# A pre-LN block in fp32 on one core: the last token block adds x in two one-pass parts, with its sums, pieces, filler and down weights on other queues and engines

## The chip, the cores and the metric

The kernel runs on one core of one Trainium2 chip. The metric is the time of one execution in device microseconds; a kernel's time is the median of its runs. The core has a matrix engine (PE), a vector engine (DVE), a scalar engine (ACT), GpSimd (POOL) and a sync engine (SP) that here only issues DMAs. Each engine works through its own list of instructions in order and waits on semaphores; ACT and POOL issue DMAs from the same lists. In the rows of the profile "PE" is a matmul, "PEld" its weight load, and "SPq", "ACTq", "POOLq" a DMA being issued.

## The reference

A pre-LN transformer block: attention with 32 query heads and one shared key and value head, then a gated feed-forward part. Sequence 2048, width D = 512, 32 heads of 16, feed-forward width F = 1792, all in fp32.

```python
def _A_ref(x, wq, wk, wv, wo):
    q = (x @ wq).reshape(B, S, H, Dh).transpose(...)
    k = x @ wk
    v = x @ wv
    p = softmax(einsum("bhqd,bkd->bhqk", q, k) * Dh ** -0.5)
    o = einsum("bhqk,bkd->bhqd", p, v)
    return o.transpose(...).reshape(B, S, H * Dh) @ wo

def _B_ref(x, w_gate, w_up, w_down):
    return (gelu(x @ w_gate) * (x @ w_up)) @ w_down

h = x + _A_ref(layernorm(x), wq, wk, wv, wo)
h2 = h + _B_ref(layernorm(h), w_gate, w_up, w_down)
```

## The kernel before

**Tiling.** The 2048 tokens are worked in NB = 4 blocks of T = 512, each of TB = 4 parts of P = 128. A block's attention runs over NG = 8 groups of four heads and KC = 16 key chunks: scores (`s`, L352), exponentials on ACT (`p`, L356) and weighing (`acc`, L360). An `acc` holds, for each of four heads, 16 rows of weighed values and 16 rows that repeat the sum of the exponentials, the divisor.

**Precision.** Matmuls take fp32r operands in one pass; full precision comes from splitting an operand into a high part, the value rounded to fp32r, and a low part, the remainder (`split`, L121: the high part by one engine, the subtraction by the same or another). A product is then hi*hi + hi*lo + lo*hi. Where an operand stays plain fp32, the trace shows two records for one matmul (eight for the four additions of x, L848). The identity `ident` (L102) is fp32; it serves the transposes and, in `add_x` (L847), puts x into the bank of the projection by a matmul of x against the identity.

**What sets the order.** Blocks 0 to 2 are pipelined: while ACT makes the exponentials of block b, a planner (`CYCLES`, L1090 to L1114) weaves in the projection, norm and feed-forward products of block b - 1. A `step` issues the next planned matmul, `available` tells how many can be issued, `catch_up` issues those that are left before a point, `before` and `finish` issue the weighing and the side work due. When fewer products are available than a cycle wants, the cycle is "idle": all available products are issued first. The lists of SP and DVE in this stretch are in program order, not rearranged by the scheduler; those of PE, POOL and ACT are in program order throughout.

**The tail.** The last block has no attention beside it. `rest` (L807) holds back 36 down matmuls of block 2 (token parts 2 and 3, 18 each) as filler for PE. `last_dense` (L818) is a generator that stops at `HOLD`; the driver at L1122 to L1132 runs 18 filler matmuls, goes on to the next HOLD, runs 9, goes on, and then issues the 9 that remain. In `last_dense`:

- L840: x of the last block is loaded into `xp`, four DMAs of 256 KB on SP; then `load_w2` (L515) for the first two pairs of down weights, `w2_3_0` and `w2_3_1`, 1 MB each on SP, into buffers of the same tag `p`.
- The projection `pp` of the first three chunks of 128 channels: 36 matmuls, 9 for each token part.
- Four pieces, one for each token part of the last chunk: `piece(t)` (L409) inverts the divisors, multiplies and splits into `o_hi`, `o_lo`, all on DVE; `add_x(t)`; three matmuls of the last chunk. After piece 2 stands the norm of part 0 (L860), after piece 3 the others. A norm is two statistics instructions on DVE (L132, L133), three small ones on POOL (`rstd`, `shift`, L135 to L143) and one on ACT (`xnp`).
- Transposes (`pxt`, L828), ACT's high part (`x2h`) and DVE's low part (`x2l`), parts 0 and 1 ahead of parts 2 and 3, which use the same two banks.
- Then the feed-forward part: per f of 14 a gate group (`pg`) and an up group (`pu`) of 12 matmuls each, with w1 weights in three buffers: the load issued when a group ends serves the group three further on. `load_w2` at L950 asks for the remaining pairs `w2_3_2` to `w2_3_6`, on SP.

**The last sums.** `evacuate` (L370) copies the last `acc` to `oT` (L373, DVE), and `move_out` (L379) brings its rows to the partitions where the pieces need them: eight DMAs of 32 KB, the divisors' half first, alternating between SP and ACT. The stores of block 2's parts 0 and 1, `out_dram<-h` (L704), are issued by SP after DVE's last h additions (L702).

Of the kernel before, what the change touches and what calls it, by code (L numbers as in the profile page):

```python
# [9 lines left out]
F32 = mybir.dt.float32  # L10
F32R = mybir.dt.float32r
# [8 lines left out]
P = 128  # L20
# [6 lines left out]
PB = 5  # L27
# [30 lines left out]
def kernel(  # L58
# [12 lines left out]
    nc = tc.nc  # L71
# [29 lines left out]

    ident = const.tile([P, P], F32, name="ident")  # L102
    make_identity(nc, ident)
    power = const.tile([P, 2], F32, name="power")
    nc.vector.memset(power[:, 0:1], -0.5)
    nc.vector.memset(power[:, 1:2], 0.5)
# [14 lines left out]
    def split(eng_hi, hi, lo, src, eng_lo=None):  # L121
        if eng_hi is nc.scalar:
            nc.scalar.activation(hi, src, AF.Copy)
        else:
            eng_hi.tensor_copy(hi, src)
        (eng_lo or nc.vector).tensor_tensor(lo, src, hi.bitcast(F32), op=ALU.subtract)
# [29 lines left out]
    def run(outer, first):  # L156
# [214 lines left out]
        def evacuate(b, g, acc):  # L371
            oT = sb.tile([P, T], F32, tag="oT", bufs=1, name=f"oT_{b}_{g}")
            nc.vector.tensor_copy(oT, acc)  # L373
            c, k = divmod(g, 2)
            if k == 0:
                pair[0] = sb.tile([P, 2, T], F32, tag="oc", bufs=2, name=f"oc_{b}_{c}")
            oc = pair[0]

            def move_out():  # L379
                for half in (1, 0):  # L380
                    for j in range(4):
                        r0, r1 = 64 * k + DH * j, 32 * j + DH * half
                        (nc.sync, nc.scalar)[j % 2].dma_start(
                            oc[r0 : r0 + DH, half, :], oT[r1 : r1 + DH, :]
                        )

            def turn_out():
                view = acc_d[:, g % 4, :].rearrange("(j s e) t -> j e s t", s=2, e=DH)
                for j in range(4):
                    r0 = 64 * k + DH * j  # L390
                    nc.sync.dma_start(oc[r0 : r0 + DH, :, :], view[j])


            def invert(t):
                sl = slice(t * P, (t + 1) * P)
                nc.vector.reciprocal(oc[:, 1, sl], oc[:, 1, sl])  # L396

            def divide():
                if c == 0:
                    o_blk[b] = [  # L400
                        sb.tile([P, DC, T], F32R, tag=f"o_{w}", bufs=1, name=f"o_{w}_{b}")
                        for w in ("hi", "lo")
                    ]
                hi, lo = o_blk[b]
                nc.vector.tensor_tensor(oc[:, 0, :], oc[:, 0, :], oc[:, 1, :], op=ALU.mult)
                split(nc.vector, hi[:, c, :], lo[:, c, :], oc[:, 0, :])


            def piece(t):  # L409
                sl = slice(t * P, (t + 1) * P)  # L410
                hi, lo = o_blk[b]
                invert(t)
                nc.vector.tensor_tensor(
                    oc[:, 0, sl], oc[:, 0, sl], oc[:, 1, sl], op=ALU.mult
                )
                split(nc.vector, hi[:, c, sl], lo[:, c, sl], oc[:, 0, sl])
                pieces[b] = t + 1

            if b == NB - 1 and g == NG - 1:
                move_out()  # L420
            else:
                nc.sync.dma_start(acc_d[:, g % 4, :], oT)
                if b == 0 and g < NG - 1:
                    outs.append([turn_out])
                else:
                    turn_out()
            if b == NB - 1 and g == NG - 1:
                last_out.append(piece)
            elif b > 0 and g == NG - 1:
                outs.extend([partial(piece, t), partial(piece, t + 1)] for t in (0, 2))  # L430
            elif k == 1:

                outs.extend([[] for _ in range(4 if b == 0 else 1)])
                outs.extend([partial(invert, t), partial(invert, t + 1)] for t in (0, 2))
                outs.append([divide])
            if b == 0 and g == NG - 1:
                while outs:
                    take_out()
                pieces[b] = TB
# [72 lines left out]
            nc.sync.dma_start(w.bitcast(F32), w1_d[f, k].bitcast(F32))  # L512
            w1s[b, f, k] = w

        def load_w2(b, j):  # L515
            if b == NB - 1 and j < 2:
                w = sb.tile([P, 2, 2, D], F32R, tag="p", bufs=PB, name=f"w2_{b}_{j}")
            else:
                w = db.tile([P, 2, 2, D], F32R, tag="w2", bufs=3, name=f"w2_{b}_{j}")
            nc.sync.dma_start(  # L520
                w.bitcast(F32), w2_d[2 * j : 2 * j + 2].rearrange("f p i d -> p f i d").bitcast(F32)
            )
            w2s[b, j] = w
# [291 lines left out]
                    yield 1  # L815
                add_down(b, t, bank, True)

        def last_dense():  # L818
            b = NB - 1
            o_hi, o_lo = o_blk[b]  # L820
            xns, hb = {}, {}
# [3 lines left out]
            def x_turn(t):  # L825
# [6 lines left out]
                    nc.vector.tensor_tensor, lo, pt, hi.bitcast(F32), op=ALU.subtract  # L832
                )

            xp, xn, h = (
                sb.tile([P, TB, D], F32, tag="p", bufs=PB, name=f"{n}p_{b}")
                for n in ("x", "xn", "h")
            )
            for t in range(TB):
                nc.sync.dma_start(xp[:, t, :], x_t[:, b * TB + t, :])  # L840
            for j in range(2):
                load_w2(b, j)

# [1 line left out]
            pps.extend(tail_bank(f"pp_{b}_{t}") for t in range(1, TB))  # L845

            def add_x(t):  # L847
                nc.tensor.matmul(pps[t], ident, xp[:, t, :], start=False, stop=False)  # L848

            def project_part(t, cs, start):  # L850
                terms = [
# [10 lines left out]
            def norm(t):  # L862
                scaled[t] = layer_norm(tiny, xns[t], pps[t], f"2_{b}_{t}", on_act=True)

            piece, scaled = last_out.pop(), {}
            for t in range(TB):
                hb[t], xns[t] = h[:, t, :], xn[:, t, :]
                project_part(t, range(DC - 1), True)
            for t in range(TB):
                piece(t)  # L870
                add_x(t)
                project_part(t, (DC - 1,), False)
                if t == 2:
                    norm(0)
            for t in range(1, TB):
                norm(t)
            for t in range(TB - 1):
# [60 lines left out]
            for fs in RUNS:  # L938
                early_f = 2 if fs is RUNS[-1] else 1
                for n, f in enumerate(fs):  # L940
                    if f % 2 == 0:
                        gs[b, f // 2] = [
                            db.tile([P, 2, T], F32R, tag=tag, bufs=3, name=f"{tag}_{b}_{f // 2}")
                            for tag in ("gh", "gl")
                        ]
                    yield from up(f, *gs[b, f // 2])
                    if n + 1 == early_f and prev is not None:
                        yield from down(prev, False)
                    for j in {3: (2,), 4: (3,), 6: (4,), 8: (5,), 10: (6,)}.get(f, ()):
                        load_w2(b, j)  # L950
                prev = fs
            yield from down(prev, True)

# [6 lines left out]
        def finish(n):  # L960
            for _ in range(min(n, len(pend))):
                pb, pg, pkc, pp, pacc, _ = pend.pop(0)
                weigh(pacc, pp, pkc)
                if pkc == KC - 1:
                    evacuate(pb, pg, pacc)
# [36 lines left out]
        with tc.manual_schedule(engines={mybir.EngineType.SP, mybir.EngineType.DVE}):  # L1002
# [19 lines left out]
            def norm():  # L1022
                nonlocal normed
                if not normed:
                    next(work)
                    normed = True
# [63 lines left out]
        for i in range(-((lead - end) // 16)):  # L1090
            if first and i in BOUND_LISTS:
                bound_flag(BOUND_LISTS.index(i))
            for count, woven, plain in CYCLES:
                idle = available() < woven.count("d")
                if idle:
                    while available():
                        step()
                    if at == len(queue) or queue[at][0].startswith("pg"):
                        catch_up()
                bent = before(idle)  # L1100
                if not idle:
                    finish(count)
                for key in bent:
                    later.extend(gate(*key))
                for move in plain if idle else woven:
                    if move == "d":
                        step()
                    elif move == "v":
                        finish(1)
                        clock += 4  # L1110
                    elif n < end:
                        score(n)
                        n += 1
                        clock += 1  # L1114
# [4 lines left out]
            tc.tile_pool(name="ps_tail", bufs=1, side="right", space=PSUM)  # L1119
        )  # L1120

        tail, filling = last_dense(), rest()  # L1122
        with tc.manual_schedule(engines={mybir.EngineType.DVE}):
            catch_up()
            side(100)
            assert next(tail) == HOLD
            for steps in (18, 9):
                for _ in range(steps):
                    next(filling)
                assert next(tail) == HOLD  # L1130
            for _ in filling:
                pass  # L1132
# [319 lines left out]
```

## Time and profile before

| | us |
|---|---|
| median of 3 runs | 1418.01 (1417.7 to 1419.28) |
| profiled execution | 1417.39 |
| its span in the trace | 1415.2 |
| PE busy | 1388.3 (98%) |
| ACT busy | 1030.1 (73%) |
| DVE busy | 632.7 (45%) |
| POOL busy | 218.3 (15%), nearly all in the first 300 us |

All times in rows count from the span's start. A row of a timeline gives start, busy time, engine, line, operation, output <- inputs with their shapes, how many were joined, and in brackets how long the engine had been idle and what ended that. A row of grouped lines gives the total busy time and the mean of one in ns, then the idle time before them. A row of windows gives the busy time of each engine in a stretch, the granted clock of PE, the busy share of the DMA engines and GB/s. A chain row gives start, duration and what the end of the kernel waited for then. Matmuls are pipelined: the ramp of one overlaps the one before, so rows of single matmuls last longer than their period.

### The profile page before, as it was taken

The numbers are of one execution on the slowest core, as the hardware profiler recorded it, in microseconds if no ns is written. First come the engines' busy times: TensorE is split into PE (matmuls) and PEld (weight loads), VectorE is DVE, ScalarE is ACT, GpSimd is POOL, SyncE is SP. The second block draws the span as 40 slices with busy tenths as digits, with TensorE's granted clock in tenths as the row PEclk, the third lists the DMA queues.
The fourth block names the chain that finished last, engine by engine and source line by source line (L and its number), as shares of the span: only waits on it lengthen the run. The fifth ranks groups of instructions, "written<-read, shape, count | busy, mean of one in ns | idle before, by whom it ended". The sixth has DMA issues, their size and how long they took to land.

```text
span 1415.2 us, 25089 instructions
## 1 busy us (share of the span) xinstructions
PE 1388.3 (98%) x10384; PEld 752.6 (53%) x10384; DVE 632.7 (45%) x1043; ACT 1030.1 (73%) x1147; POOL 218.3 (15%) x305
## 2 busy tenths in 40 slices
PE   6999999999999999999999999999999999999998
PEld 5533333335455555555555555545555555557886
DVE  7412221214364354454354454445264453536665
ACT  6699999997777777777777777787778777752000
POOL 5576866630000000000000000000000000001000
PEclk9999999999999999999999999999999999999999
DMA  4466766645222333311432333311333332344352
GB/s 158 135 210 204 225 211 214 213 151 199 78 85 93 116 102 117 102 65 57 153 105 87 118 116 101 102 65 36 141 101 102 117 101 102 105 141 171 131 190 77
DMA packets 66850, 180.31 MB, mean 127 GB/s; under 512 B 9484, under 2 KB 9484, under 8 KB 66696
## 3 DMA queue, kind: packets, MB, share of 16 engines
q1 hardware_dynamic: 56768, 144.40, 31.0%
q0 software_dynamic: 9760, 34.08, 7.5%
q8 instruction: 84, 1.38, 0.4%
q14 instruction: 38, 0.31, 0.1%
q10 hardware_dynamic: 200, 0.14, 0.0%
HBM read 130.87 MB, written 47.45 MB: 126 GB/s over the span
## 4 chain that ended last, share of the span: by engine, by line
PE 93%; ACT 2%; DMA 1%; DVE 1%; issue 1%; SPq 0%; DVEq 0%; ACTq 0%
PE acc L360 32%; PE s L352 20%; PE pg L772 8%; PE pu L772 8%; PE pd L772 8%; PE pq L205 4%; PE pd L802 3%; PE pp L772 2%; PE pu L802 2%; PE pg L802 2%; ACT p L356 2%; DMA w<-w_d 1%; PE pk L1240 1%; PE pd_rest L814 1%; PE pxt L598 0%
## 5 line engine op out<-in xcount | busy, mean ns | idle before, releaser
L356 ACT ACTIVATE p<-s 128x1024 f32<-128x1024 f32 x1024 | 959.3, 1040 | 231.0 <-PE s L352 230.7
L360 PE MATMUL acc<-p,v_sb 128*32 128x512 f32 x4096 | 490.0, 598 | 0.0
L352 PE MATMUL s<-qg,kaug 50*128 50x512 f32 x1984 | 386.8, 427 | 4.0 <-ACT p L356 3.6
L352 PEld LDWEIGHTS s<-qg,kaug 50*128 50x128 f32 x1984 | 170.7, 184 | 287.8 <-issue 131.3
L360 PEld LDWEIGHTS acc<-p,v_sb 128*32 128x32 f32 x4096 | 110.2, 109 | 228.9 <-issue 215.7
L772 PE MATMUL pg<-x2h,w 64*128 64x512 f32 x672 | 173.8, 392 | 0.0
L772 PE MATMUL pu<-x2h,w 64*128 64x512 f32 x672 | 172.7, 391 | 0.0
L135 POOL TENSOR_SCALAR rstd<-mv 128x1 f32<-128x1 f32 x16 | 3.5, 220 | 964.8 <-DVE mv L133 964.7
L772 PE MATMUL pd<-w,gh 64*128 64x512 f32 x624 | 123.9, 392 | 1.4 <-DVE h L702 1.4
L702 DVE TENSOR_TENSOR h<-h,pd 128x512 f32<-128x512 f32 x80 | 54.4, 686 | 148.0 <-PE pd L772 148.0
L772 PEld LDWEIGHTS pg<-x2h,w 64*128 64x128 f32 x672 | 94.3, 185 | 11.9
L772 PEld LDWEIGHTS pu<-x2h,w 64*128 64x128 f32 x672 | 94.5, 186 | 11.0
L772 PE MATMUL pg<-x2l,w 64*128 64x512 f32 x336 | 99.3, 391 | 0.0
L772 PE MATMUL pu<-x2l,w 64*128 64x512 f32 x336 | 99.1, 391 | 0.0
L772 PEld LDWEIGHTS pd<-w,gh 64*128 64x128 f32 x624 | 68.2, 185 | 13.4 <-DVE h L702 2.7
L911 ACT ACTIVATE ga<-ga 128x512 f32<-128x512 f32 x14 | 8.8, 632 | 90.4 <-DVE ga L908 90.4
L396 DVE RECIPROCAL oc<-oc 128x128 f32<-128x128 f32 x64 | 56.6, 922 | 34.5 <-DMA oc<-acc_d 27.3
L772 PE MATMUL pd<-w,gl 64*128 64x512 f32 x312 | 71.8, 391 | 0.0
L639 DVE TENSOR_TENSOR g<-g,pg 128x512 f32<-128x512 f32 x42 | 28.8, 685 | 90.5 <-PE pg L772 90.5
L635 DVE COPY g<-pg 128x512 f32<-128x512 f32 x42 | 29.0, 692 | 72.2 <-PE pg L772 72.2
L639 DVE TENSOR_TENSOR u<-u,pu 128x512 f32<-128x512 f32 x42 | 28.8, 686 | 68.3 <-PE pu L772 68.3
L373 DVE COPY oT<-acc 128x512 f32<-128x512 f32 x32 | 22.1, 691 | 72.4 <-PE acc L360 72.4
(244 smaller groups left out, 1459.2 us busy)
## 6 DMA issues: line engine op xcount, KB each, us to landing
w<-w_d SPq DMA_DIRECT2D x112, 512.0 KB
w<-w_d SPq DMA_DIRECT2D x28, 1024.0 KB
qg<-q_d SPq DMA_DIRECT2D x62, 200.0 KB
q_d<-qh SPq DMA_DIRECT2D x32, 256.0 KB
acc_d<-oT SPq DMA_DIRECT2D x31, 256.0 KB
oc<-acc_d SPq DMA_DIRECT2D x124, 64.0 KB
w_d<-w_0b POOLq DMA_DIRECT2D x14, 512.0 KB, 5.8
w_d<-w_1b POOLq DMA_DIRECT2D x14, 512.0 KB, 6.3
```

Source lines behind the costliest of these rows:

```text
L205: nc.tensor.matmul(pq, wt[:, d, c * P : (c + 1) * P], xt[:, d, :], start=(n == 0), stop=(n == 3 * DC - 1),)
L352: nc.tensor.matmul(s[:, a, :], kaug[rows, kc * P : (kc + 1) * P], qg[rows, u, :], start=True, stop=True,)
L356: nc.scalar.activation(p[:, 2 * u : 2 * u + 2, :], s, AF.Exp, scale=SCALE)
L360: nc.tensor.matmul(acc[32 * j : 32 * j + 32, :], v_sb[:, kc, :], p[:, j, :], start=(kc == 0), stop=(kc == KC - 1), skip_group_check=True,)
L373: nc.vector.tensor_copy(oT, acc)
L396: nc.vector.reciprocal(oc[:, 1, sl], oc[:, 1, sl])
L635: nc.vector.tensor_copy(half, bank)
L639: nc.vector.tensor_tensor(half, half, bank, op=ALU.add)
L702: nc.vector.tensor_tensor(hs[b, t], hs[b, t], bank, op=ALU.add)
L772: nc.tensor.matmul(bank, lhsT[r], rhs[r], start=(k == 0), stop=(k == n - 1), skip_group_check=True,)
L802: nc.tensor.matmul(bank, lhsT, rhs, start=(i == 0), stop=(i == len(ts) - 1))
L814: nc.tensor.matmul(bank, lhsT, rhs, start=(i == 0), stop=(i == len(ts) - 1))
```

## The change

The whole diff:

```diff
--- before.py
+++ after.py
@@ -101,6 +101,8 @@
 
     ident = const.tile([P, P], F32, name="ident")
     make_identity(nc, ident)
+    ident_r = const.tile([P, P], F32R, name="ident_r")
+    nc.vector.tensor_copy(ident_r, ident)
     power = const.tile([P, 2], F32, name="power")
     nc.vector.memset(power[:, 0:1], -0.5)
     nc.vector.memset(power[:, 1:2], 0.5)
@@ -380,7 +382,7 @@
                 for half in (1, 0):
                     for j in range(4):
                         r0, r1 = 64 * k + DH * j, 32 * j + DH * half
-                        (nc.sync, nc.scalar)[j % 2].dma_start(
+                        (nc.gpsimd, nc.scalar)[j % 2].dma_start(
                             oc[r0 : r0 + DH, half, :], oT[r1 : r1 + DH, :]
                         )
 
@@ -413,7 +415,10 @@
                 nc.vector.tensor_tensor(
                     oc[:, 0, sl], oc[:, 0, sl], oc[:, 1, sl], op=ALU.mult
                 )
-                split(nc.vector, hi[:, c, sl], lo[:, c, sl], oc[:, 0, sl])
+                if b == NB - 1:
+                    split(nc.scalar, hi[:, c, sl], lo[:, c, sl], oc[:, 0, sl], nc.gpsimd)
+                else:
+                    split(nc.vector, hi[:, c, sl], lo[:, c, sl], oc[:, 0, sl])
                 pieces[b] = t + 1
 
             if b == NB - 1 and g == NG - 1:
@@ -512,12 +517,12 @@
             nc.sync.dma_start(w.bitcast(F32), w1_d[f, k].bitcast(F32))
             w1s[b, f, k] = w
 
-        def load_w2(b, j):
+        def load_w2(b, j, queue=nc.sync):
             if b == NB - 1 and j < 2:
                 w = sb.tile([P, 2, 2, D], F32R, tag="p", bufs=PB, name=f"w2_{b}_{j}")
             else:
                 w = db.tile([P, 2, 2, D], F32R, tag="w2", bufs=3, name=f"w2_{b}_{j}")
-            nc.sync.dma_start(
+            queue.dma_start(
                 w.bitcast(F32), w2_d[2 * j : 2 * j + 2].rearrange("f p i d -> p f i d").bitcast(F32)
             )
             w2s[b, j] = w
@@ -815,7 +820,24 @@
                     yield 1
                 add_down(b, t, bank, True)
 
-        def last_dense():
+        x_parts = []
+
+        def prepare_x():
+            b = NB - 1
+            xp = sb.tile([P, TB, D], F32, tag="p", bufs=PB, name=f"xp_{b}")
+            for t in range(TB):
+                nc.sync.dma_start(xp[:, t, :], x_t[:, b * TB + t, :])
+            for t in range(TB):
+                if t % 2 == 0:
+                    xhi = sb.tile([P, 2, T], F32R, tag="qg", bufs=2, name=f"xhi_{t}")
+                xlo = db.tile([P, T], F32R, tag=("g", "ga")[t // 2], bufs=2, name=f"xlo_{t}")
+                split(
+                    nc.scalar, xhi[:, t % 2, :], xlo, xp[:, t, :],
+                    (nc.gpsimd, nc.vector)[t % 2],
+                )
+                x_parts.append((xhi[:, t % 2, :], xlo))
+
+        def last_dense(filling):
             b = NB - 1
             o_hi, o_lo = o_blk[b]
             xns, hb = {}, {}
@@ -832,12 +854,10 @@
                     nc.vector.tensor_tensor, lo, pt, hi.bitcast(F32), op=ALU.subtract
                 )
 
-            xp, xn, h = (
+            xn, h = (
                 sb.tile([P, TB, D], F32, tag="p", bufs=PB, name=f"{n}p_{b}")
-                for n in ("x", "xn", "h")
+                for n in ("xn", "h")
             )
-            for t in range(TB):
-                nc.sync.dma_start(xp[:, t, :], x_t[:, b * TB + t, :])
             for j in range(2):
                 load_w2(b, j)
 
@@ -845,7 +865,8 @@
             pps.extend(tail_bank(f"pp_{b}_{t}") for t in range(1, TB))
 
             def add_x(t):
-                nc.tensor.matmul(pps[t], ident, xp[:, t, :], start=False, stop=False)
+                for part in x_parts[t]:
+                    nc.tensor.matmul(pps[t], ident_r, part, start=False, stop=False)
 
             def project_part(t, cs, start):
                 terms = [
@@ -867,11 +888,13 @@
                 hb[t], xns[t] = h[:, t, :], xn[:, t, :]
                 project_part(t, range(DC - 1), True)
             for t in range(TB):
+                add_x(t)
+            for t in range(TB):
                 piece(t)
-                add_x(t)
                 project_part(t, (DC - 1,), False)
-                if t == 2:
-                    norm(0)
+                for _ in range(2):
+                    next(filling)
+            norm(0)
             for t in range(1, TB):
                 norm(t)
             for t in range(TB - 1):
@@ -947,7 +970,7 @@
                     if n + 1 == early_f and prev is not None:
                         yield from down(prev, False)
                     for j in {3: (2,), 4: (3,), 6: (4,), 8: (5,), 10: (6,)}.get(f, ()):
-                        load_w2(b, j)
+                        load_w2(b, j, nc.gpsimd)
                 prev = fs
             yield from down(prev, True)
 
@@ -1098,6 +1121,8 @@
                     if at == len(queue) or queue[at][0].startswith("pg"):
                         catch_up()
                 bent = before(idle)
+                if n == end and not x_parts:
+                    prepare_x()
                 if not idle:
                     finish(count)
                 for key in bent:
@@ -1106,6 +1131,8 @@
                     if move == "d":
                         step()
                     elif move == "v":
+                        if n == end and not x_parts:
+                            prepare_x()
                         finish(1)
                         clock += 4
                     elif n < end:
@@ -1119,12 +1146,13 @@
             tc.tile_pool(name="ps_tail", bufs=1, side="right", space=PSUM)
         )
 
-        tail, filling = last_dense(), rest()
+        filling = rest()
+        tail = last_dense(filling)
         with tc.manual_schedule(engines={mybir.EngineType.DVE}):
             catch_up()
             side(100)
             assert next(tail) == HOLD
-            for steps in (18, 9):
+            for steps in (12, 9):
                 for _ in range(steps):
                     next(filling)
                 assert next(tail) == HOLD
```

- `ident_r` is an fp32r copy of the identity. `prepare_x` loads x of the last block and splits it, the high parts `xhi` on ACT, the low parts `xlo` on POOL (parts 0 and 2) and DVE (parts 1 and 3). The planner's loop calls it once, when all scores have been issued, before the last weighing. `add_x` becomes two one-pass matmuls for each part, and all four additions stand ahead of the first piece.
- `move_out` issues from POOL and ACT in place of SP and ACT.
- In the pieces DVE keeps the reciprocal and the product; ACT makes `o_hi` and POOL `o_lo`.
- After each piece's three matmuls two filler matmuls are issued. All norms stand behind the four pieces. The driver then runs 12, 9 and the remaining 7 fillers.
- `w2_3_2` to `w2_3_6` are issued by POOL in place of SP.

## The prediction

> **What bounds the kernel now.** The page's busy times and its chain come first, then the chain of waits from 1262 us on, since all changed work but one small copy lies behind it.
>
> ```profile
> PE 1388.3 (98%) x10384; PEld 752.6 (53%) x10384; DVE 632.7 (45%) x1043; ACT 1030.1 (73%) x1147; POOL 218.3 (15%) x305
> PE 93%; ACT 2%; DMA 1%; DVE 1%; issue 1%; SPq 0%; DVEq 0%; ACTq 0%
> ```
>
> PE holds the end, so a change to the last block is worth only the PE idle time or PE work that it removes there.
>
> ```profile
> 1265.90 0.70 DVE h L702
> 1266.62 0.34 SPq L704
> ...
> 1267.06 6.12 DMA w<-w_d
> 1273.19 1.87 DMA oc<-oT
> ...
> 1282.90 4.10 PE pd_rest L814 x18
> ...
> 1292.89 2.73 PE pg L802 x12
> 1295.64 5.69 DMA w<-w_d
> ```
>
> From 1267 to 1275 the chain leaves PE: SP's store, the 1 MB load `w2_3_1` behind it (6.12 us), then the last 32 KB of sums (1.87 us). PE does the projection of the first three chunks meanwhile. I measure the change by two times: R, the start of the first reciprocal of the last chunk, and T0, the start of the first up group, 1292.73 by its first matmul (the chain's 1292.89 leaves its ramp out). SP's order, and ACT's moves of the sums:
>
> ```profile
> 1257.88 1.76 SPq L840 DMA_DIRECT2D xp<-in_A_x_dram  x4
> 1259.73 0.38 SPq L520 DMA_DIRECT2D w<-w_d  x1
> 1265.64 1.32 SPq L704 DMA_DIRECT2D out_dram<-h  x2
> 1267.06 0.38 SPq L520 DMA_DIRECT2D w<-w_d  x1
> 1268.50 5.19 SPq L383 DMA_DIRECT2D oc<-oT  x4
> 1268.51 2.45 ACTq L383 DMA_DIRECT2D oc<-oT  x4
> ```
>
> x is asked for at 1257.88, nine microseconds before the stores of block 2 are done with SP. The sums leave at 1268.5, and:
>
> ```profile
> 1267.79 0.69 DVE L373 COPY oT<-acc 128x512 f32<-128x512 f32 x1 [1.20 <-PE acc L360]
> 1273.97 0.95 DVE L396 RECIPROCAL oc<-oc 128x128 f32<-128x128 f32 x1 [5.50 <-DMA oc<-oT]
> 1281.92 0.50 PE L857 MATMUL pp<-wo_hi,o_hi 128*128 128x512 f32 x1 [0.29 <-DVE o_hi L125]
> 1301.46 0.70 PE L802 MATMUL pu<-x2h,w 128*128 128x512 f32 x2 [0.41 <-DMA w<-w_d]
> 1373.28 2.09 PE L802 MATMUL pu<-x2h,w 128*128 128x512 f32 x8 [0.46 <-DMA w<-w_d]
> ```
>
> R is 1273.97, T0 is R + 18.76. DVE is idle 5.50 us before R, yet PE loses only 0.29 us in the pieces, and later 0.41 and 0.46 us at two w1 loads. That 1.16 us is all the waiting of PE that I can point to here.
>
> **The change part by part.**
>
> *One-pass x.* The four adds of x in fp32 become eight passes.
>
> ```profile
> 1275.95 1.02 PE L848 MATMUL pp<-xp,ident 128*128 128x512 f32 x2
> ...
> 1277.51 1.02 PE L848 MATMUL pp<-xp,ident 128*128 128x512 f32 x2
> ```
>
> The period of an add with its three one-pass matmuls is 1.56 us; a one-pass matmul is 2.73 / 12 = 0.228 us (the chain's up group), so an add is 1.56 - 0.68 = 0.87 us. Four cost 3.49, eight passes 1.82: PE's work falls by 1.66 us. The copy of the identity at the start is a 128x128 cast on DVE (0.23 us, below) beside the first loads; I take 0, and 0.25 us if nothing hides it.
>
> *What making x ahead moves.* The built program puts SP's four loads of x behind both stores of block 2, since the planner issues all block-2 products that are left before it calls the new function. The second store waits for the h add that ends at 1266.59, so x is asked for at 1266.96 instead of 1257.88, 9.1 us later, and `w2_3_0` and `w2_3_1` follow at once (1.76 us of issue for x, 0.38 each): at 1268.7 and 1269.1. Nothing large precedes them any more. On DVE, `xlo_1` and `xlo_3` stand ahead of the copy of the last sums, oT; on ACT the four `xhi` copies, and on POOL two `xlo`, stand ahead of their DMAs of the sums. So the last sums now wait for the last of x. Traffic in that time:
>
> ```profile
> DMA packets 421, 1.27 MB, mean 295 GB/s; under 512 B 32, under 2 KB 32, under 8 KB 421
> ## 3 DMA queue, kind: packets, MB, share of 16 engines
> q1 hardware_dynamic: 421, 1.27, 93.6%
> ...
> 1295.60:1301.30 5.70, 5.45 (x25) 4.17 (x23) 4.71 (x8) 0.63 (x1) 0.00 (x0) 1.00 0.97 359
> ```
>
> The first three rows are the DMA view of 1267 to 1271.3 us (295 GB/s, and no packet of ACT's queue q10), the last the window of 1295.6 to 1301.3 (359 GB/s). Stores (2 x 256 KB) and x (4 x 256 KB), 1.57 MB, take 5.3 us at 295 GB/s; moving from about 1267.6, a microsecond after the stores' issue (an estimate), x is there at 1272.9, at 359 GB/s at 1272.0. Then `xhi_3` and `xlo_3`:
>
> ```profile
> L123 ACT ACTIVATE wq_hi<-wq_raw x4: 612/614/619, 16.1 to 23.8; 128x512 fp32r<-128x512 f32 x4
> ...
> L126 POOL TENSOR_TENSOR wq_lo<-wq_raw,wq_hi 128x512 fp32r<-128x512 f32 x4 | 5.1, 1284 | 2.4 <-ACT wq_hi L123 2.4
> ```
>
> 0.61 us on ACT, 0.69 on DVE (the size of the oT copy; POOL's two, 1.28 each, end earlier since their x is loaded earlier), 0.2 for the waits, then oT 0.69: oT is ready at about 1275.1 (1274.2 to 1276), 6.6 us later than the 1268.48 of now.
>
> *The sums on ACT and POOL.* The four on SP waited for a DMA slot of `w2_3_1` (the 4th goes at 1273.19); that is gone. POOL issues in about 0.57 us each, as ACT does (2.45 / 4 = 0.61), so the two sides of the divisors leave by 1276.3 and land 1.87 us later: R = 1278.2 if no load delays them. But now 3.67 MB (stores, x, two w2) are queued from 1267.6 on, done at 1277.8 (359 GB/s) to 1280.0 (295). The trace says how a small move fares behind such a load: ACT's four were issued from 1268.51, none of their packets moved before 1271.3, when q1 had nearly done its megabyte, and the reciprocal that needs two of them began at 1273.97 instead of about 1271.6 (1268.51 + 1.2 + 1.87), 0.8 us after `w2_3_1` had landed (1267.06 + 6.12). I take the same here, 0.8 us after the middle of the loads' end, 1278.9: R = 1279.7, bounds 1278.0 (no waiting) and 1281 (295 GB/s).
>
> *From R to T0.* Costs:
>
> ```profile
> L396 DVE RECIPROCAL oc<-oc 128x128 f32<-128x128 f32 x4 | 3.8, 942 | 5.5 <-DMA oc<-oT 5.5
> L413 DVE TENSOR_TENSOR oc<-oc 128x128 f32<-128x128 f32 x4 | 1.2, 293 | 0.4 <-DMA oc<-oT 0.3
> L126 DVE TENSOR_TENSOR o_lo<-oc,o_hi 128x128 fp32r<-128x128 f32 x4 | 1.2, 292 | 0.1
> L125 DVE CAST o_hi<-oc 128x128 fp32r<-128x128 f32 x4 | 0.9, 227 | 0.1
> ...
> 1283.74 0.67 DVE L132 BATCH_NORM_STATS2 st<-pp 128x6 f32<-128x512 f32 x1
> 1284.44 0.18 DVE L133 BATCH_NORM_AGGREGATE mv<-st 128x2 f32<-128x6 f32 x1
> ...
> 1284.42 0.22 POOL L135 TENSOR_SCALAR rstd<-mv 128x1 f32<-128x1 f32 x1
> ...
> 1285.73 0.22 POOL L135 TENSOR_SCALAR rstd<-mv 128x1 f32<-128x1 f32 x1
> ...
> 1285.69 0.78 ACT L878 ACTIVATE xnp<-pp,shift,rstd 128x512 f32<-128x512 f32 x1 [0.54 <-POOL shift L143]
> 1287.47 0.60 ACT L881 ACTIVATE x2h<-pxt 128x512 fp32r<-128x512 f32 x1 [1.01 <-PE pxt L828]
> ```
>
> A piece holds DVE for 0.94 + 0.29 = 1.24 us, 1.75 before. The last product is at R + 4.95, then a quarter-size split, scaled from the two full-size rows with half as floor (ACT 0.3, POOL 0.5 us), and three matmuls: R + 6.3. All four norms now stand behind the pieces: the first statistics end at R + 5.8, one follows each 0.8 us, and POOL's part takes 1.31 us each (1284.42 to 1285.73), so POOL paces: shifts at R + 7.2, 8.5, 9.8, 11.1. ACT normalizes blocks 0, 1, 2 by R + 10.6, evicts the turned block 0 (11.2), normalizes block 3 (12.0), evicts block 1 (12.6). DVE's low part of block 1 ends at R + 13.4; the last turned block uses its bank and ends at R + 13.8; seven filler matmuls (1.6) follow: T0 = R + 15.4, 3.4 us less than now. The 18, 9 and 9 fillers that covered the norms are 8, 12, 9 and 7 now; PE idles beside POOL and ACT and not only behind R.
>
> T0 = 1279.7 + 15.4 = 1295.1, **2.4 us later**, bounds 0.7 (R = 1278.0) and 3.7 (R = 1281).
>
> *w2 on POOL.* `w2_3_4`, issued by SP behind two w1 loads (about 6 us into the up groups), now leaves as soon as its buffer is free, near T0, on POOL's queue, with 2 MB of w1 and w2 in flight while the w1 load that gave 0.41 us is due. If it is shared evenly the stall stays or goes (-0.4); if the w1 load waits behind it, 1.05 MB at 359 GB/s is up to 2.9 us. POOL's other queue moved beside SP's in the weight phase, so I take 0 here. At 1373 the two w2 loads leave when they did, on another queue than the w1 load: -0.3 of the 0.46.
>
> **Sum:** 2.4 - 0.3 = +2.1 us. The profiled execution took 1417.39 us (span 1415.2 and 2.2 around it), 0.62 under the median, so 1419.5 on its own footing and **1420.1** against the median of 1418.01.
>
> **The rivals.** *The loads don't hold up the sums.* If ACT's and POOL's queues get their turn at once, R = 1278.0 and T0 moves by 0.7, with the 0.3 above 1418.4: no change. Against it stands q10's silence until 1271.3. This is what the Trainium skill would give ("DMA: Bandwidth & Descriptors", "Queues, rings and completion order": each engine takes queue rows in turn, packet by packet); the trace disagrees on when the packets move, though that section's other rule, that a completion is written only behind all earlier writes of its engine, agrees with late landings.
>
> *PE sets the end and the late sums are hidden.* Then the 1.66 us of x and the 0.29 us go, T0 is 1290.8, and with both w1 stalls gone the time is 1418.0 - 1.95 - 0.87 = 1415.2. For it: PE's work really shrinks and DVE's pieces too. Against: it needs R by 1275.4 (1290.8 - 15.4), hence oT by 1272.3, before the last of x is there.
>
> *The early `w2_3_4` holds back the w1 load:* 2.9 us on top, 1423.0. It decides once the load lands more than 8.2 us (three up groups of 2.72) behind T0. For it: 5.69 us was already 0.41 too long. Against: another queue.
>
> *PE loses its clock in the gap.* PE has its x adds done by about 1277.8 and gets the first piece at R + 1.8: 3.6 us idle. If the clock were halved for as long, 1.8 us more: 1421.8. The only row on it:
>
> ```profile
> 1380.00:1415.00 35.00, 28.92 (x128) 23.63 (x126) 18.08 (x28) 1.90 (x3) 0.00 (x0) 0.99 0.23 78
> ```
>
> PE stands idle for its last 6 us, and a granted clock of 0.99 allows half speed for only about 0.7 of them: the drop came some 5 us into the gap, so 3.6 should pass. The Trainium skill ("TensorE: Matmul & The Clock Gate", "Part 1: The HAM clock gate") puts half speed after an idle window of about 3.4 us, which this gap would just exceed.
>
> **How the numbers follow.** Forecast 0.45 (own range 1418.5 to 1422), turn-taking 0.18, PE sets the end 0.15, w1 held back 0.14, clock 0.08. A measurement tells 0.2% (2.8 us) from no change: faster is below 1415.2, slower above 1420.8. Faster: most of the 0.15, 0.13. Slower: 0.18 of the forecast's 0.45, 0.14, and 0.06 of the clock: 0.38. The rest, 0.49, is no change. The range leaves out the better half of the PE case and the worst of the w1 case: 1415.4 to 1423.2.
>
> **What would show it.** Right: x issued near 1267; the oT copy behind `xlo_3` near 1275; R near 1279.7 with a PE gap of 3 to 4 us ahead of the first piece; T0 near R + 15.4 and shifts of POOL 1.31 us apart. Wrong: oT ready by 1272, R under 1277, a granted clock under 0.95 in 1276 to 1296, or a w1 stall over a microsecond in the first up groups.

## The result and the profile after

The changed kernel takes 1427.87 us (median of 6 runs, 1424.86 to 1430.65) where the kernel before takes 1417.86 (6 runs on the same chip): ratio 1.0068, 95% interval 1.0058 to 1.0078, about 10 us slower. That is above the forecast of 1420.1 and above its range of 1415.4 to 1423.2. The profiled execution took 1426.17 us, its span is 1424.4, 9.2 more than before.

The chain of waits of the changed kernel, its last block (start, duration, what the end waited for):

```profile
1266.23 0.70 DVE h L707
...
1268.77 4.39 DMA xp<-in_A_x_dram
1273.19 0.64 ACT xhi L125
...
1274.85 0.69 DVE oT L375
1275.59 8.96 PE pp L878 x27
1284.54 1.86 PE pp L869 x8
1286.40 0.70 PE pp L878 x3
...
1290.57 3.22 PE pd_rest L819 x14
...
1299.22 2.73 PE pg L807 x12
1301.97 7.41 DMA w<-w_d
1309.52 3.01 PE pu L807 x12
...
1382.46 3.01 PE pu L807 x12
```

Four steps can be read off against the chain of before. The last h addition starts 0.33 us later (1266.23 against 1265.90), before the change has done anything here. The first up group starts 6.33 us later (1299.22 against 1292.89). The first `pu` that waits for its w1 weights is 8.06 us behind (1309.52 against 1301.46), the second 9.18 (1382.46 against 1373.28). So the last block lost 6.0 us and the two w1 waits 1.7 and 1.1.

What fills the 6.0 us stands in a row of PE's timeline and in the windows around it (busy time of PE, PEld, DVE, ACT, POOL, then the granted clock, the busy share of the DMA engines, GB/s):

```profile
1269.92 0.39 PE L878 MATMUL pp<-wo_hi,o_lo 128*128 128x512 f32 x1
1275.59 0.80 PE L878 MATMUL pp<-wo_hi,o_hi 128*128 128x512 f32 x1 [5.27 <-DVE oT L375]
```

```profile
1274.20:1275.50 1.30, 0.00 (x0) 0.00 (x0) 1.30 (x2) 0.00 (x0) 0.18 (x1) 0.50 1.01 413
1275.60:1281.00 5.40, 5.40 (x13) 4.24 (x14) 0.85 (x1) 0.00 (x0) 2.05 (x4) 0.50 0.57 184
1281.10:1286.00 4.90, 4.90 (x22) 3.98 (x22) 3.76 (x8) 1.25 (x4) 1.84 (x4) 1.00 0.00 0
```

PE does the nine products of token part 0 and then stands for 5.27 us. The other 27 products of the first three chunks write into the tail's own banks, which the kernel opens in place of those of `acc` and the scores, and the first of the 27 waits for the oT copy, the last reader of `acc`. While PE stands its granted clock falls to 0.50, and it stays there for 5.4 us of work. 5.27 of waiting and 5.4 x 0.50 = 2.7 of slow clock, less the 1.66 us of the x additions and the 0.29 us of waiting in the pieces that are gone, make 6.0.

The copy of the sums and their DMAs came close to the working:

```profile
1274.85 0.68 DVE L375 COPY oT<-acc 128x512 f32<-128x512 f32 x1
1280.15 0.95 DVE L398 RECIPROCAL oc<-oc 128x128 f32<-128x128 f32 x1 [4.62 <-DMA oc<-oT]
```

### The profile page after: what moved, and what is told of

The parts are those of the page before. It is cut to its first block, busy times and chain, and to the rows that moved or that the text cites. A ratio compares the mean times of both kernels' runs of the same rounds, so it can differ in the third digit from the quotient of the medians.

```text
span 1424.4 us, 25126 instructions
## 1 busy us (share of the span) xinstructions
PE 1389.7 (98%) x10384; PEld 754.5 (53%) x10384; DVE 635.0 (45%) x1038; ACT 1033.7 (73%) x1155; POOL 229.7 (16%) x320
## 4 chain that ended last, share of the span: by engine, by line
PE 93%; ACT 3%; DVE 1%; issue 1%; DMA 1%; SPq 0%; POOL 0%; ACTq 0%; DVEq 0%
PE acc L362 32%; PE s L354 20%; PE pu L777 8%; PE pg L777 8%; PE pd L777 8%; PE pq L207 4%; PE pd L807 3%; ACT p L358 3%; PE pp L777 2%; PE pu L807 2%; PE pg L807 2%; PE pk L1268 1%; PE pp L878 1%; PE pd_rest L819 1%; DMA w<-w_d 1%
## 5 line engine op out<-in xcount | busy, mean ns | idle before, releaser
L127 DVE CAST qh<-pq 128x512 fp32r<-128x512 f32 x11 | 7.6, 690 | 112.0 <-PE pq L207 112.0
```

## Experiments

Each kernel was run beside the kernel before on the same chip. The times of chips differ by a microsecond or two (1417.9 to 1419.7 for the kernel before), so ratios to the kernel before are compared; 0.1% is 1.4 us. A ratio is one of medians, while rows and spans come from a single profiled run. e11 was run once and has no ratio.

| run | ratio to before | 95% interval |
|---|---|---|
| changed kernel | 1.0068 | 1.0058 to 1.0078 |
| e1_hold_clock | 1.0033 | 1.0021 to 1.0046 |
| e2_w2_on_sp | 1.0053 | 1.0041 to 1.0065 |
| e3_before_w2_on_pool | 1.0032 | 1.0023 to 1.0041 |
| e4_x_behind_sums | 1.0005 | 0.9996 to 1.0014 |
| e5_x_behind_sums_w2_sp | 0.9989 | 0.9980 to 0.9997 |
| e6_before_x_early | 1.0040 | 1.0027 to 1.0052 |
| e7_x_on_pool_queue | 1.0050 | 1.0037 to 1.0063 |
| e8_before_x_behind_sums | 1.0006 | 0.9997 to 1.0015 |
| e9_w2_in_calm | 0.9978 | 0.9969 to 0.9987 |
| e10_filler_in_gap | 1.0041 | 1.0028 to 1.0055 |

**The slow clock alone (e1).** PE gets dummy work in its gap and nothing else changes.

```diff
+                for _ in range(18 if t == 0 else 0):
+                    nc.tensor.matmul(pps[0], o_hi[:, 0, 0:P], wo_hi[:, 0, :], start=True, stop=True)
                 project_part(t, range(DC - 1), True)
```

> The changed kernel with 18 extra one-pass matmuls (each its own closed group, overwritten by the first real product) ahead of the first token part's products, so that PE works 4.1 us of its 5.3 us gap. Theory (the gap costs twice: idle time, and afterwards 5.4 us at half clock): granted clock stays 1.00 through the last block, the copy of the last sums and R stay near 1275.5 and 1280.2, the start of the first up group comes 2.7 us earlier, total 1425.2. Rival (the end is paced by R and the POOL norms, the clock only uses up slack): clock 1.00 too, but the first up group starts within 0.7 us of the changed kernel's, total 1427.2 to 1428.

Its windows, its chain and its row of the wait:

```profile
1275.60:1281.00 5.40, 5.40 (x25) 4.45 (x24) 0.77 (x1) 0.00 (x0) 1.66 (x4) 1.00 0.48 125
```

```profile
1274.98 6.43 PE pp L878 x27
...
1296.09 2.73 PE pg L807 x12
```

```profile
1274.98 0.50 PE L878 MATMUL pp<-wo_hi,o_hi 128*128 128x512 f32 x1 [1.26 <-DVE oT L375]
```

The clock is 1.00 in the same stretch, the 27 products take 6.43 us instead of 8.96, and the last h addition (1265.55 here) to the first up group is 30.5 us instead of 33.0: 2.5 us from the clock alone, 2.7 expected. The chain runs through PE's own work to the first up group, so PE sets the end of the block and not R and the norms; but it comes at R + 15.7 here (1295.93 by its first matmul, R 1280.23), and if PE had been done sooner, the norms would have held the group back to about R + 15.4 by the working, only 0.3 us earlier. The ratio fell by 0.35%, 5 us, more than the clock's part. In the profiled run the two w1 waits were smaller as well (1.33 and 0.57 us, 1.8 us less in all); why they are is not known.

**Where x is made (e4, e6, e7).** In e4 the new function is called at the start of `last_dense`, so behind the evacuation.

```diff
-                if n == end and not x_parts:
-                    prepare_x()
...
+            prepare_x()
             xn, h = (
```

> The changed kernel with x loaded and split at the start of the last block's code, so behind the copy of the last sums on DVE and behind their DMAs on ACT and POOL; everything else as changed. Theory (27 projection matmuls wait for the bank that the copy of the last sums frees; PE pays the wait, then the clock): no PE wait on that copy, clock 1.00, first up group near 1291 instead of 1299.2, the w1 waits of about 2.1 and 1.6 us stay, total 1418 to 1419.5. Rival (the chain from R over POOL's norms paces the end whichever way the copy goes): first up group at R + 15.4 or later, above 1294, total above 1421.

```profile
1266.87 1.85 PE acc L362 x16
1268.72 8.40 PE pp L879 x36
1277.12 1.86 PE pp L870 x8
1278.98 0.70 PE pp L879 x3
...
1291.80 2.73 PE pg L807 x12
```

The chain of e4 is PE's without a break: 24.9 us from the last weighing to the first up group, where the kernel before has 27.1 (its weighing starts at 1265.79). The last block is now 2.2 us better than before, and the ratio falls from 1.0068 to 1.0005, 9 us. What is left over is the w1 waits (2.14 and 1.91 us) and a stretch at half clock behind the second (its row is in the last section).

e6 adds to the kernel before only the preparation at the changed kernel's place, with one-pass additions.

```diff
                 bent = before(idle)
+                if n == end and not x_parts:
+                    prepare_x()
...
+                        if n == end and not x_parts:
+                            prepare_x()
                         finish(1)
```

> The kernel before with the new preparation of x alone, at the changed kernel's place, and its one-pass additions; sums, pieces, filler and w2 as before. Theory (this place alone makes the loss in the last block): PE waits about 5.3 us for the copy of the last sums, half clock follows, the first up group starts about 6 us later than in the kernel before, total +6 us. Rival (the other parts are needed for it): total within 3 us of the kernel before.

```profile
1276.81 0.80 PE L875 MATMUL pp<-wo_hi,o_hi 128*128 128x512 f32 x1 [5.19 <-DVE oT L375]
```

The wait is the same, 5.19 us, and the ratio is 1.0040: 5.7 us slower, 6 expected. The place is enough by itself.

e7 keeps the changed kernel's place but has POOL issue the loads of x.

```diff
-                nc.sync.dma_start(xp[:, t, :], x_t[:, b * TB + t, :])
+                nc.gpsimd.dma_start(xp[:, t, :], x_t[:, b * TB + t, :])
```

> The changed kernel with the four loads of x issued by POOL instead of SP, nothing else. Theory (the order on DVE does no harm by itself; x is late because its loads stand behind the stores of block 2 on SP): x is there by 1266, the copy of the last sums ends within 1.5 us of the last weighing, no PE wait on it, clock 1.00 in the last block, total as with x behind the sums: 0.5 to 1.5 us above the kernel before. Rival (the split itself in front of the copy costs the time): the copy ends 3 us or more after the last weighing and PE waits for it, total 4 us or more above the kernel before.

```profile
1258.77 2.24 POOL L829 DMA_DIRECT2D xp<-in_A_x_dram  x4 [269.70 <-ACT p L358]
```

```profile
1259.11 1.23 SPq L525 DMA_DIRECT2D w<-w_d  x2
1266.02 1.32 SPq L709 DMA_DIRECT2D out_dram<-h  x2
```

```profile
1269.88 0.63 ACT L125 ACTIVATE xhi<-xp 128x512 fp32r<-128x512 f32 x1 [2.05 <-DMA xp<-in_A_x_dram]
```

x was asked for at 1258.77, but SP, freed of it, sent both w2 megabytes ahead of the stores at 1259.11, and the last quarter of x, loaded beside them, was there only at 1269.9. The oT copy ended at 1271.83, 3.7 us behind the last weighing, PE waited 1.54 us for it at full clock, and the total is 7.1 us above the kernel before. So the rival's numbers came, but its reason only in part: from the arrival of the last quarter of x to the end of DVE's last `xlo` it is 1.4 us, and x itself was late. With x off SP the wait of PE fell from 5.27 to 1.54 us. Since the w2 loads moved too, it is inferred and not shown that the loads beside x made what was left, and a run in which only DVE's two `xlo` stand behind the oT copy was not made.

The last block lost nothing in the profiled run: 26.1 us from the end of the last h addition to the first up group, 26.3 before. The ratio of 1.0050 comes from behind it: the w1 waits were 2.98 and 1.76 us, 3.9 us more than before, and from the last addition to the end of the span it took 7.6 us instead of 5.6, which stays unexplained.

**w2 on POOL (e2, e3).** e2 takes the queue argument out of the changed kernel, e3 puts it into the kernel before.

```diff
-                        load_w2(b, j, nc.gpsimd)
+                        load_w2(b, j)
```

> The changed kernel with w2_3_2 to w2_3_6 issued by SP again. Theory (POOL's queue sends w2_3_4 ahead of the w1 loads and holds them back): the two waits of PE for w1 go from 2.14 and 1.56 us back to about 0.4 and 0.5, total 1425.1 (-2.8). Rival (the waits come from the later and closer start of w2_3_2 and w2_3_3 in the new tail, whichever queue they take): waits stay above 1.5 us, total within 1 us of 1427.9.

> The kernel before with w2_3_2 to w2_3_6 issued by POOL and nothing else. Theory (queue and early start are enough): the waits for w1 grow from 0.41 and 0.46 to about 2.1 and 1.6 us, total 1420.7 (+2.8). Rival (they need the new tail): waits below 1 us each, total within 1 us of 1417.9.

PE's waits for w1 in the profiled runs (the rows of two of them, the second of the changed kernel and the first of e7, name an instruction of DVE or ACT on `ga` that had just ended; the products do not read `ga`, and their w1 load was under way until about then, so they are counted here as well):

| run | w2 issued by | first, us | second, us |
|---|---|---|---|
| before | SP | 0.41 | 0.46 |
| changed kernel | POOL | 2.14 | 1.56 |
| e2_w2_on_sp | SP | 0.76 | 0.57 |
| e3_before_w2_on_pool | POOL | 3.38 | 0.91 |
| e4_x_behind_sums | POOL | 2.14 | 1.91 |
| e7_x_on_pool_queue | POOL | 2.98 | 1.76 |

The row of e3's first wait, its three loads on POOL, and its windows during the wait and behind it:

```profile
1304.36 3.17 PE L802 MATMUL pu<-x2h,w 128*128 128x512 f32 x8 [3.38 <-DMA w<-w_d]
```

```profile
1289.75 0.80 POOL L520 DMA_DIRECT2D w<-w_d  x1 [2.87 <-PE pd_rest L814]
1291.74 0.72 POOL L520 DMA_DIRECT2D w<-w_d  x1 [1.19 <-PE pd_rest L814]
1293.12 0.71 POOL L520 DMA_DIRECT2D w<-w_d  x1 [0.65 <-PE pd_rest L814]
```

```profile
1300.60:1304.30 3.70, 0.37 (x2) 0.00 (x0) 2.94 (x5) 0.63 (x1) 0.00 (x0) 1.00 1.03 420
1305.10:1308.30 3.20, 3.20 (x9) 2.43 (x8) 0.00 (x0) 0.00 (x0) 0.00 (x0) 0.50 0.03 13
```

In e3 nothing but the queue differs from the kernel before: `w2_3_4` goes at 1293.1, 0.3 us behind the first up group, where SP sent it 5.9 us behind it. The DMA engines are full during the wait (420 GB/s), and the clock drops behind it. It costs 0.32%, 4.5 us, where 2.8 were expected. In the profiled runs the two waits grew by 3.4 us and 3.2 us of work at half clock cost 1.6, which the expectation left out; together they are the 5.0 us between the spans (1420.2 and 1415.2). In the changed kernel the same edit undone (e2) gives 2.4 us of the waits back in the profiled runs. Its time is 0.15% lower, but the intervals overlap (1.0041 to 1.0065 against 1.0058 to 1.0078), so the times alone do not show it.

**Both undone (e5), and x alone (e8).** e5 is e4 and e2 together. e8 is the kernel before with one-pass x made behind the sums, without the new pieces and filler.

> The changed kernel with both moves undone: x made behind the copy of the last sums, and w2_3_2 to w2_3_6 on SP. Theory (PE work less 1.66 us for x and 0.3 us of waiting, w1 waits back at 0.4 to 0.6 us): the first up group starts 24.9 us after the last weighing instead of 27.1, total 2.0 us under the kernel before. Rival (the early w2 loads were a gain and SP's place for them costs): total no better than the run with w2 on POOL, 0.8 us above the kernel before.

> The kernel before with one-pass x alone, prepared behind the copy of the last sums. Theory (without filler between the pieces PE waits for DVE's pieces of 1.78 us each, which the fp32 additions had filled): the 1.66 us are given back as PE waits between the pieces, total between -0.3 and +1.2 us of the kernel before. Rival (less PE work is less time): total 1.6 us under the kernel before.

e5 runs at 0.9989 of the kernel before, 1.6 us faster (2.0 expected). Its up groups start 24.9 us behind the last weighing, as expected, but its w1 waits are 2.7 us in all, on SP's queue too, where 0.4 to 0.6 were expected of each:

```profile
PE pu L807 <- DMA w<-w_d: 1.9, 2, 1.0
PE pg L807 <- DMA w<-w_d: 0.8, 1, 0.8
```

(waits of PE: us in total, times, longest.) So POOL's queue is not the only way to them. The shorter block less these waits makes 0.4 us, which is what the profiled spans differ by (1414.8 and 1415.2); why the medians differ by more is open.

e8 runs at 1.0006. PE waits 0.24, 0.35, 0.33 and 1.15 us in its four pieces, 2.1 us, and the first matmul behind each wait lasts 0.50 us instead of 0.39. That eats the 1.66 us of x and more: the first up group comes 1.0 us later behind the last weighing than in the kernel before. In e5, with filler and faster pieces, the same x pays.

**w2 away from w1 (e9).** From e5; the loads of `w2_3_2` and `w2_3_3` go into buffers of tag `p` and are issued by ACT behind the pieces, the other three stand ahead of a down phase, and SP's list in the tail is in program order (the lines below leave that part of the edit out).

```diff
-            if b == NB - 1 and j < 2:
+            if b == NB - 1 and j < 4:
...
+            for j in (2, 3):
+                load_w2(b, j, nc.scalar)
             norm(0)
...
+                    for j in {4: (4, 5, 6)}.get(f, ()):
+                        load_w2(b, j)
                     if n + 1 == early_f and prev is not None:
                         yield from down(prev, False)
-                    for j in {3: (2,), 4: (3,), 6: (4,), 8: (5,), 10: (6,)}.get(f, ()):
-                        load_w2(b, j)
```

> The run with x behind the sums and w2 on SP, with its w2 loads moved away from the w1 loads: w2_3_2 and w2_3_3 take buffers of tag p and are issued by ACT behind the pieces, when no DMA is under way; w2_3_4 to w2_3_6 are issued by SP in one go ahead of the first down phase, which needs no w1; SP's list in the tail is in program order. Theory (the w1 waits come from w2 megabytes in flight at the same time, whatever the queue): no w1 wait above 0.3 us, total 1.0 to 2.0 us under that run, 2.5 to 3.5 us under the kernel before. Rival (the w1 load needs its 5.5 us anyway): waits of 0.4 us or more stay, total within 0.7 us of that run.

```profile
1290.60 2.72 PE pg L807 x12
1293.32 2.72 PE pu L807 x12
1296.04 2.72 PE pg L807 x12
1298.76 1.36 PE pu L807 x6
```

```profile
1280.00 0.92 ACTq L525 DMA_DIRECT2D w<-w_d  x2
```

No wait of PE for w1 is left in its trace; the two loads went at 1280.0, in a stretch in which the kernel before moves nothing. Its ratio is 0.9978, 3.1 us faster than the kernel before: a version that beats both. The program order of SP was not tried without the moves.

**Filler in the gap (e10).** The changed kernel with 18 fillers behind part 0's products.

```diff
                 project_part(t, range(DC - 1), True)
+                for _ in range(18 if t == 0 else 0):
+                    next(filling)
...
-            for steps in (12, 9):
+            for steps in (4, 3):
```

> The changed kernel with 18 of its 36 filler matmuls issued behind the first token part's products, so in PE's gap, and 8, 4, 3 and 3 left for later. Theory (PE's idle time and its half clock are the loss of the last block): wait on the copy of the last sums 1.2 us, clock 1.00, the norms through POOL now set the end of the block, first up group at R + 13.4, about 1293.6 instead of 1299.2, total 5 to 6 us under the changed kernel. Rival (the moved filler is missed later by as much): first up group not before 1296.1, total no better than 3 us under the changed kernel, as with dummy work in the gap.

The chain of its profiled run:

```profile
1290.74 0.71 PE pp L878 x3
1291.47 0.71 DVE st L134
...
1295.12 0.23 POOL rstd L137
...
1296.43 0.23 POOL rstd L137
...
1299.73 0.66 PE pxt L850 x4
1300.39 0.70 PE pd_rest L819 x3
1301.09 3.00 PE pg L807 x12
```

The ratio is 1.0041, 3.8 us under the changed kernel, between the two theories. The profiled run is the longest of its five (1427.94), and half clock shows in it again behind a wait of 1.79 us, so the expected 1.00 did not hold. Here POOL's norms do set the end, 1.31 us apart, and the first up group is at R + 16.3 (R 1284.77), 13.4 expected. PE, slowed by the clock, was done with its products and additions only at 1290.74, so the first statistics ended at R + 7.6 and not at the working's R + 5.8: 1.8 of the 2.9 us.

**Low parts of x on DVE alone (e11).** From e5, run once.

```diff
-                    (nc.gpsimd, nc.vector)[t % 2],
+                    nc.vector,
```

> The run with x behind the sums and w2 on SP, with all four low parts of x on DVE. Theory (DVE and POOL slow each other when both subtract fp32 tiles in SBUF): each of DVE's four takes 0.69 us instead of 1.5, the four together 2.8 us against 3.07 for two. Rival (an SBUF operand pair of this shape always takes DVE 1.3 to 1.5 us): four take 5.3 us or more. Time of the kernel within its noise of that run in either case, by the first.

DVE's rows of e11 and of e4, in that order:

```profile
1271.75 2.50 DVE L128 TENSOR_TENSOR xlo<-xp,xhi 128x512 fp32r<-128x512 f32 x4 [3.25 <-ACT xhi L125]
```

```profile
1273.26 3.07 DVE L128 TENSOR_TENSOR xlo<-xp,xhi 128x512 fp32r<-128x512 f32 x2 [3.78 <-ACT xhi L125]
```

DVE does four in 2.50 us where it took 3.07 for two: the theory's numbers came. The one time, 1418.44, tells nothing of what the kernel gains.

## Why the prediction was wrong

- **PE's work in the gap: the step that failed.** The working kept "PE does the projection of the first three chunks meanwhile" from the kernel before, and the clock rival said that PE has its x adds done by about 1277.8; in the trace they end at 1286.4. The delay of oT was followed only along the sums, through R. But oT also frees a bank: 27 of the 36 products stood behind it, at no cost before since the copy was done at 1268.48, before part 0's nine products ended. The traces show a PE wait of 5.27 us ahead of these products, where none was counted; e4 takes the wait away and gains 9 us, e6 adds it to the kernel before and loses 5.7.
- **The clock.** That case was named with 0.08 and a price of 1.8 us for 3.6 us of idling. The gap came earlier and was longer, and the price was 2.5 to 2.7 us (e1). The end-of-kernel row was read as a threshold near 5 us; e3, e10 and e11 show half clock behind waits of 3.38, 1.79 and 2.33 us. The Trainium skill ("TensorE: Matmul & The Clock Gate", "Part 1: The HAM clock gate") has half clock after an idle window of about 3.4 us, and this window runs freely and does not restart with the kernel. The gaps of 5.0 to 5.3 us here (e2, e6, the changed kernel) agree; those of 1.79 to 2.33 us cannot hold a full idle window, and half clock followed all the same.
- **oT and R were right, R in part by luck.** oT was ready at 1275.5 (forecast 1275.1), R was at 1280.15 (1279.7), and x was asked for at 1267.38. One term in it was small: DVE's last `xlo` took 1.08 us and not 0.69, since it ran beside POOL's. Of the 4.6 us from oT to R the working gave 3.1 to the way of the sums and 1.5 to the loads. In e7, with the big loads landed, it took 3.6 us and POOL's moves of the sums landed in 2.4 us, 3.6 in the changed kernel: so the loads were worth about 1.0 us (an estimate from these two runs) and the way was longer than counted.
- **T0 = R + 15.4 was wrong in kind.** T0 came at R + 18.9 (1299.06 by its first matmul), since PE and not POOL set the end. Where POOL did (e10), the pace of 1.31 us was right. In e4 the first up group does lie at R + 15.4 (1276.25 to 1291.64), but its chain is PE's alone: there the number fits by luck.
- **w1 behind `w2_3_4`** was a rival at 0.14 and up to 2.9 us, for the first load; the forecast took 0 there and a gain of 0.3 at the second. Measured: +1.7 and +1.1 us in the profiled run, and in the kernel before (e3) 4.5 us in all. The ground given for the 0, two queues that move side by side, did not help: in e3 the DMA engines were full during the wait (420 GB/s).
- **The gain was real.** The x additions save what was counted: without the wait the block is 2.2 us shorter (e4, e5), close to 1.66 + 0.29 = 1.95.

In sum: +0.3 before the block, +6.0 in it (forecast +2.4), +2.8 at the w1 loads (forecast -0.3).

## What to carry to other kernels

When a copy out of a matmul bank moves, list everything that the copy releases: the bank's next writer stands in no chain of before as long as the copy is early. Beside the stall itself, price a slow clock behind it: here it followed every stall of PE above 3 us and some of those of about 2 us. Bulk loads belong in a stretch where nothing short is awaited; moving them to another queue did not give them one here.

## What the runs showed of the hardware

- Half clock can follow a PE wait of only 1.79 us (e10, from 1282.3 on, 1.5 us after PE had resumed) and be absent behind 2.98 us (e7) and 2.14 us (e4: 1.00 from 1302.1 to 1309.0, then 0.50 behind its second wait of 1.91 us). The length of the wait alone did not decide it. The row and window of e10, then the two windows of e4:

```profile
1280.81 0.50 PE L878 MATMUL pp<-wo_hi,o_hi 128*128 128x512 f32 x1 [1.79 <-DVE oT L375]
1282.30:1285.60 3.30, 3.30 (x9) 2.59 (x8) 0.83 (x1) 0.00 (x0) 0.79 (x2) 0.50 0.37 80
```

```profile
1302.10:1309.00 6.90, 6.90 (x31) 5.72 (x32) 3.81 (x7) 0.63 (x1) 0.00 (x0) 1.00 0.42 137
1376.50:1379.70 3.20, 3.20 (x9) 2.47 (x8) 0.52 (x1) 0.00 (x0) 0.00 (x0) 0.50 0.05 13
```

- DVE and POOL slow each other when both subtract 128x512 fp32 tiles of x: 1.5 us each on DVE and on POOL beside the other (e4), about 0.63 each on DVE alone (e11) and 1.29 on POOL alone (e7). The ends look like turns taken by whole instructions: in e4 POOL's first ends at 1274.08, DVE's first at 1274.63, POOL's second at 1275.78 and DVE's second at 1276.32, so each ends 0.5 to 1.2 us behind the other engine's, about what it takes alone or less. POOL's row of e4:

```profile
1272.79 2.99 POOL L128 TENSOR_TENSOR xlo<-xp,xhi 128x512 fp32r<-128x512 f32 x2 [0.98 <-ACT xhi L125]
```
